# A fused attention and gated-MLP kernel: TensorE's warm-up in short matmuls, and the output weights loaded earlier

## The chip, the cores and the metric

The kernel runs on one core of a Trainium2 chip. The metric is the device time of one execution in microseconds, from start to end. All times below are microseconds unless marked ns. Five engines work side by side, each through its own queue of instructions: TensorE (PE, with its weight loads shown as a row of their own, PEld), VectorE (DVE), ScalarE (ACT), GpSimd (POOL) and SyncE (SP), which in this kernel issues nearly all DMAs.

## What is computed

Two branches read the same normalised input, and the input is added to their sum. S is 2048 rows, D is 640 columns.

```python
xn = layernorm(x)                                  # no scale, no shift
# A: 32 heads of 20 columns, each query sees the 256 keys up to its own
q, k, v = split(xn @ wqkv)
p = softmax(where(0 <= i - j < 256, q @ k.T * 20 ** -0.5, -1e9))
a = (p @ v) @ wo
# B: gated MLP with 1536 hidden columns
b = (sigmoid(xn @ w_gate) * (xn @ w_up)) @ w_down
out = x + a + b                                    # bfloat16
```

## The kernel before

The rows are worked in four chunks of 512 (`NCH`, `CW`). For each chunk the kernel normalises the rows and turns them (xnT, features on partitions); projects Q and K (`proj_block`, L334) and stores them to a scratch in DRAM, from which `spread` (L352) reads them back with the heads placed on partitions 0, 32, 64 and 96; projects V (L364); computes gate and up products (L454, L461) and h; the scores of step after step (`scores`, L530: 16 to 32 small matmuls a step, then one exponential on ACT and masks on POOL); the products with V (`pv`, L561: some 96 small matmuls); and the output sums, down projection (L475) and output projection (L482) into the same PSUM tile, to which DVE adds the input (L486).

PE's order of work is written out by hand. A list of 75 score steps is walked (15 in chunk 0, 20 in each later chunk, five for each pair of head groups); between two steps a `Fill` object hands out other work, piece by piece, from generators that are queued in a fixed order (`qk1`, `v1`, `out0`, `qk2`, ...), by costs in nanoseconds. Every other engine's queue, SP's too, gets its instructions in the order in which this Python program calls them, and runs them in that order; each waits on semaphores for what it needs. SP's DMAs take turns on eight semaphores, so an issue also waits until the DMA eight places ahead of it has landed.

Three places matter for the change.

*The start.* `keep_warm` (L244) issues matmuls of a constant (ones) into a PSUM tile that nothing reads. Ten of 512 columns stand first in PE's queue. Then come the five transposes of row block 0 (L302, `transpose_rows`), which need the block normalised by DVE (L295), one more warm-up matmul, the transposes of row block 1 (normalised by L669), and the first sums, the V projections (L364). Every matmul is two instructions on PE, a weight load and the matmul itself. The warm-up takes two of the four PSUM buffers of the pool `ps_d`.

*Chunk 1's loads.* `g_v(1)` projects V for chunk 1, four row blocks s, and issues loads as it goes: after s = 0 the first half of K (two spreads), after s = 1 the second halves of Q and of K (`spread`, two DMAs of 256 KB each, four in all), after s = 2 `load_wo` (L223), the output weights in twelve small DMAs (L226, L228, L231) of 40 to 100 KB. The second halves are first read in chunk 1's eleventh score step, the output weights by the first output projection of chunk 0 (L482, in `out0`). Behind them in SP's queue stand the stores of chunk 2's normalised rows (L306), the residual rows for `out0` (L492) and the reads of the normalised rows (L313).

*PE's instructions themselves.* The program is unrolled: PE runs 8,717 instructions (8,690 without the waits and branches that stand by themselves), which reach the core by a DMA queue of their own, in packets of 16 KB.

## Time and profile before

| | us |
|---|---|
| median of 3 runs | 309.78 |
| the three runs | 309.49, 309.78, 310.4 |
| the profiled execution | 309.91 |
| its span, first to last instruction | 307.69 |
| TensorE's clock at full speed from | 4.83 |
| first transposes, first V projection | 5.38, 6.81 |
| chunk 1's second halves issued | 73.84 to 75.86 |
| output weights issued, first use of the last of them | 75.89 to 86.8, 89.34 |
| second halves first read | 112.6 |

The profile is of one execution. A row of the timeline has the start, the time that it covers, engine, line, operation, the tiles that it writes and reads, their shape and how many instructions are merged; in brackets stands the idle time of the engine just before and what ended it. The view of the chain follows the work that ended last back from the end and says for each stretch which engine, DMA or issue it went through. The view by stretches gives busy time and count for each engine, then the granted clock of TensorE as a share of full speed, the busy share of the DMA engines and GB/s. A matmul's row includes its latency, so a stream of matmuls is best read by the distance from start to start.

### The profile page before, as it was taken

The numbers are of one execution on the slowest core, as the hardware profiler recorded it, in microseconds if no ns is written. First come the engines' busy times: TensorE is split into PE (matmuls) and PEld (weight loads), VectorE is DVE, ScalarE is ACT, GpSimd is POOL, SyncE is SP. The second block draws the span as 40 slices with busy tenths as digits, with TensorE's granted clock in tenths as the row PEclk, the third lists the DMA queues.
The fourth block names the chain that finished last, engine by engine and source line by source line (L and its number), as shares of the span: only waits on it lengthen the run. The fifth ranks groups of instructions, "written<-read, shape, count | busy, mean of one in ns | idle before, by whom it ended". The sixth has DMA issues, their size and how long they took to land.

```text
span 307.7 us, 10021 instructions
## 1 busy us (share of the span) xinstructions
PE 300.1 (98%) x4309; PEld 168.1 (55%) x4344; DVE 179.8 (58%) x356; ACT 197.4 (64%) x194; POOL 164.2 (53%) x304
## 2 busy tenths in 40 slices
PE   7999999999999999999999999999999999999996
PEld 3654444555657654554457654554546665444774
DVE  5735567889856669683827465382733627372433
ACT  6823868688865648888656538868585547778000
POOL 3020668479883728676572727557382756557000
PEclk9999999999999999999999999999999999999999
DMA  7997979445655154564001222640000200000202
GB/s 203 361 344 242 324 217 285 132 150 163 181 162 133 60 161 140 183 206 84 2 2 47 65 75 92 201 150 2 2 0 4 76 33 23 2 2 2 87 21 66
DMA packets 40148, 36.03 MB, mean 117 GB/s; under 512 B 9001, under 2 KB 39849, under 8 KB 40105
## 3 DMA queue, kind: packets, MB, share of 16 engines
q1 hardware_dynamic: 39240, 34.63, 36.8%
q10 hardware_dynamic: 864, 0.77, 0.9%
q8 instruction: 34, 0.56, 0.8%
q14 instruction: 10, 0.07, 0.1%
HBM read 24.77 MB, written 10.62 MB: 115 GB/s over the span
## 4 chain that ended last, share of the span: by engine, by line
PE 91%; DMA 4%; SPq 1%; issue 1%; ACT 1%; DVE 0%
PE y L475 16%; PE pg L454 16%; PE pu L461 16%; PE pqk L334 14%; PE ps L530 8%; PE y L482 7%; PE pv L364 7%; PE acc L561 6%; DMA kT<-sk 3%; DMA wo<-in_A_wo_dram 1%; DMA xc<-in_A_x_dram 1%; SPq L231 1%; SPq L352 0%; PE pt L302 0%; ACT xn L658 0%
## 5 line engine op out<-in xcount | busy, mean ns | idle before, releaser
L542 POOL TENSOR_SCALAR_AFFINE_SELECT pT<-pT 64x512 bf16<-64x512 bf16 (+1 forms) x252 | 152.7, 606 | 91.6 <-ACT pT L535 80.0
L535 ACT ACTIVATE pT<-ps 128x2048 bf16<-128x2048 f32 x75 | 140.8, 1877 | 59.9 <-PE ps L530 58.9
L465 DVE SCALAR_TENSOR_TENSOR h<-th,pu 128x512 bf16<-128x512 f32 x48 | 32.7, 682 | 56.8 <-PE pu L461 43.0
L461 PE MATMUL pu<-xnT,wu 128*128 128x512 bf16 x230 | 58.9, 380 | 0.7 <-issue 0.3
L454 PE MATMUL pg<-xnT,wg 128*128 128x512 bf16 x225 | 58.3, 380 | 1.2 <-issue 0.6
L475 PE MATMUL y<-wd,h 128*128 128x320 bf16 (+2 forms) x396 | 56.6, 295 | 0.0
L334 PE MATMUL pqk<-xnT,wqkv 128*128 128x512 bf16 x190 | 45.1, 381 | 0.8 <-issue 0.4
L475 PEld LDWEIGHTS <-h 128*128 128x128 bf16 x396 | 36.7, 98 | 15.9 <-issue 2.2
L457 ACT ACTIVATE th<-pg 128x512 f32<-128x512 f32 x48 | 28.6, 596 | 15.3 <-PE pg L454 15.1
L454 PEld LDWEIGHTS <-wg 128*128 128x128 bf16 x240 | 22.3, 98 | 25.6 <-issue 2.0
L461 PEld LDWEIGHTS <-wu 128*128 128x128 bf16 x240 | 22.1, 98 | 25.4 <-issue 1.8
L334 PEld LDWEIGHTS <-wqkv 128*128 128x128 bf16 x200 | 22.5, 119 | 18.8 <-issue 1.2
L530 PE MATMUL ps<-qT,kT 20*64 20x320 bf16 (+4 forms) x1456 | 32.2, 259 | 0.5 <-issue 0.5
L530 PEld LDWEIGHTS <-kT 20*64 20x64 bf16 x1456 | 15.8, 103 | 25.0 <-issue 23.0
L573 DVE STREAM_TRANSPOSE t<-acc 128x512 f32<-128x512 f32 x32 | 21.1, 694 | 13.8 <-PE acc L561 13.8
L486 DVE SCALAR_TENSOR_TENSOR rows<-y,rows 128x320 bf16<-128x320 f32 x30 | 14.2, 483 | 22.5 <-PE y L482 19.7
L364 PE MATMUL pv<-wqkv,xnT 128*128 128x320 bf16 x160 | 25.9, 300 | 0.0
L482 PE MATMUL y<-wo,oc 128*128 128x320 bf16 (+2 forms) x165 | 24.4, 295 | 0.1
L561 PE MATMUL acc<-pT,v 64*32 64x320 bf16 (+4 forms) x1456 | 19.6, 252 | 0.0
L561 PEld LDWEIGHTS <-v 64*32 64x32 bf16 x1456 | 16.3, 91 | 5.8 <-ACT pT L535 1.2
L585 DVE TENSOR_TENSOR on<-t,rec 128x320 bf16<-128x320 f32 (+1 forms) x32 | 18.6, 581 | 1.1
L364 PEld LDWEIGHTS <-xnT 128*128 128x128 bf16 x160 | 14.5, 98 | 8.7 <-issue 1.2
(51 smaller groups left out, 175.3 us busy)
## 6 DMA issues: line engine op xcount, KB each, us to landing
qT<-sq SPq DMA_DIRECT2D x16, 256.0 KB
kT<-sk SPq DMA_DIRECT2D x16, 256.0 KB
sq<-st SPq DMA_DIRECT2D x20, 128.0 KB
sk<-st SPq DMA_DIRECT2D x20, 128.0 KB
out_dram<-rows SPq DMA_DIRECT2D x15, 160.0 KB
wg<-in_B_w_gate_dram SPq DMA_DIRECT2D x4, 480.0 KB
wu<-in_B_w_up_dram SPq DMA_DIRECT2D x4, 480.0 KB
xc<-in_A_x_dram SPq DMA_DIRECT2D x3, 640.0 KB
```

The lines of the kernel that those rows point to most:

```text
L334: nc.tensor.matmul(ps, lhsT=wt[:, m, :], rhs=xnT[c][:, d, :], start=(d == 0), stop=(d == DC - 1))
L364: nc.tensor.matmul(ps[:, 0:HALF], lhsT=xnT[c][:, d, s * P:(s + 1) * P], rhs=wqkv[:, d, 2 * D + hf * HALF:2 * D + (hf + 1) * HALF], start=( ...
L454: nc.tensor.matmul(pg, lhsT=part(wg, d, f), rhs=xnT[c][:, d, :], start=(d == 0), stop=(d == DC - 1))
L457: nc.scalar.activation(out=th, in_=pg, func=TANH, scale=0.5)
L461: nc.tensor.matmul(pu, lhsT=part(wu, d, f), rhs=xnT[c][:, d, :], start=(d == 0), stop=(d == DC - 1))
L465: nc.vector.scalar_tensor_tensor(out=h, in0=th, scalar=1.0, in1=pu, op0=ADD, op1=MULT)
L475: nc.tensor.matmul(y[:, 0:cut[1] - cut[0]], lhsT=ht[c, f][:, s * P:(s + 1) * P], rhs=wd[:, f, cut[0]:cut[1]], start=(f == 0), stop=False)
L482: nc.tensor.matmul(y[:, 0:cut[1] - cut[0]], lhsT=oc[c, m][:, s * P:(s + 1) * P], rhs=wo[:, m, cut[0]:cut[1]], start=False, stop=(m == DC - 1))
L530: nc.tensor.matmul(ps[a * U:(a + 1) * U, i, col * U:(col + n) * U], lhsT=qk["k", kc, o // GH][32 * i:32 * i + DH, o % GH + a, kb * U:(kb + ...
L535: nc.scalar.activation(out=pt[:, :, 0:CW], in_=ps, func=EXP, scale=SCALE)
L542: nc.gpsimd.affine_select(out=view, in_=view, pattern=[[0, HG], [0, n], [sign, U]], compare_op=GE, fill=0.0, base=base, channel_multiplier ...
L561: nc.tensor.matmul(acc[32 * i:32 * i + 32, q * U:(q + n) * U], lhsT=vt[kb][a * U:(a + 1) * U, u, h * VW:h * VW + 32], rhs=pt[a * U:(a + 1) ...
```

## The change

The warm-up becomes 2 matmuls of 512 columns and 34 of 128 ahead of the first transposes (before: 10 of 512), and 7 of 128 between the first and the second transposes (before: 1 of 512). They all write one PSUM tile instead of two. On PE 64 instructions more (32 weight loads and 32 matmuls) stand ahead of the first sums, and one more semaphore wait; from there on PE's order is the same. `load_wo` is called in chunk 1 after s = 1 instead of s = 2, and there the second halves' spreads follow after s = 2 instead of s = 1. In SP's queue the twelve loads change places with the four spreads behind the first half of K; all else keeps its place. Chunks 2 and 3, which do not load the output weights, are unchanged, and so are DVE's, ACT's and POOL's queues.

```diff
-    warm = []
-
-    def keep_warm(n):
-        if len(warm) < 2:
-            warm.append(ps_d.tile([P, CW], FP32, name="pwarm", tag="d"))
+    warm = ps_d.tile([P, CW], FP32, name="pwarm", tag="d")
+
+    def keep_warm(n, width=P):
         for k in range(n):
-            nc.tensor.matmul(warm[-1], lhsT=ones[:, 0:P], rhs=ones, start=(k == 0), stop=(k == n - 1))
-
-    keep_warm(6)
-    keep_warm(4)
+            nc.tensor.matmul(warm[:, 0:width], lhsT=ones[:, 0:P], rhs=ones[:, 0:width], start=(k == 0), stop=(k == n - 1))
+
+    keep_warm(2, CW)
+    keep_warm(34)
...
-            if c == 1 and s == 2:
+            if c == 1 and s == 1:
                 load_wo()
-            if s == 1:
+            if s == (2 if c == 1 else 1):
                 spread("q", c, GH, NG)
                 spread("k", c, GH, NG)
...
-    keep_warm(1)
+    keep_warm(7)
```

## The prediction, made before the changed kernel had run

> **What bounds the kernel now.** I read the page first (busy shares, chain), then the chain and the engines' timelines around the three places that the change touches, then the DMA queues.

> ```profile
> PE 300.1 (98%) x4309; PEld 168.1 (55%) x4344; DVE 179.8 (58%) x356; ACT 197.4 (64%) x194; POOL 164.2 (53%) x304
> ...
> q8 instruction: 34, 0.56, 0.8%
> ...
> PE 91%; DMA 4%; SPq 1%; issue 1%; ACT 1%; DVE 0%
> ```

> PE is busy for 98% of the span and is 91% of the chain: only time in which PE stands still can be won, and anything that delays PE is paid in full. PE's start-to-start times show few such stops: the first 6.8 us, one stop at the output weights, one at 203.8 us. The rest of the "issue" entries are short matmul groups with records missing (216 ns, one matmul). The profiled execution took 309.91 us (span 307.69, 2.22 around it), 0.13 above the median of 309.78. By about 0.3% (0.93 us) this kernel can be told from no change.

> **Part 1: the warm-up.** PE's timeline at the start:

> ```profile
> 0.84 4.27 PE L248 MATMUL pwarm<-const-bfloat16-1.0 128*128 128x512 bf16 x10 [0.84 <-PEq L831]
> 5.38 0.45 PE L302 MATMUL pt<-ident,xn 128*128 128x128 bf16 x5 [0.27 <-DVE xn L295]
> 5.67 0.38 PE L248 MATMUL pwarm<-const-bfloat16-1.0 128*128 128x512 bf16 x1
> 6.52 0.45 PE L302 MATMUL pt<-ident,xn 128*128 128x128 bf16 x5 [0.47 <-DVE xn L669]
> ```

> The ten warm-up matmuls start 427 ns apart (512 columns in a slow clock); the clock record goes to 1.0 at 4.83 us. They end by 5.11, the transposes wait for DVE until 5.33 (they start at 5.38, 56 ns apart, each with its own weight load), the second five wait until 6.47. So PE isn't what decides here. The new warm-up is 2 of 512 (0.85 us, to 1.69) and 34 of 128, each with a weight load. In the slow clock 128 columns are a quarter of 427, 107 ns, if the load hides. That no row shows directly; the nearest are these loads:

> ```profile
> 1.65 0.15 PEld L248 LDWEIGHTS <-const-bfloat16-1.0 128*128 128x128 bf16 x1 [0.28 <-issue]
> ...
> 5.38 0.28 PEld L302 LDWEIGHTS <-xn 128*128 128x128 bf16 x5 [1.02 <-DVE xn L295]
> ```

> A load of 147 ns begins with the matmul before it and ends well inside it; in the fast clock five follow in 0.28 us although one takes 98. So a slow pair costs 107 to 147 ns. At 107: until 4.83, 29.3 pairs; the other 4.7 at 56 ns end at 5.09. At 147: 21.4 pairs, then 12.6 x 56 ns, end 5.54, first transposes 0.16 late, which the wait for DVE's second block (6.47) covers, as 5.54 + 0.28 + 7 x 0.056 = 6.21. The seven short ones between the transposes are 0.39 us where one of 0.22 stood, and fit between 5.67 and 6.47. Cost: 0, hidden by the normalisation chain on DVE and ACT; without that cover 0.16 to 0.3. One PSUM tile is allotted instead of two; the four buffers rotate by one and no wait appears. The gain is also 0: the clock was full before the first transpose. [...]

> **Part 2: the output weights.** SP's queue in chunk 1, and the chain there:

> ```profile
> 73.84 0.98 SPq L352 DMA_DIRECT2D qT<-sq  x2
> 74.86 0.98 SPq L352 DMA_DIRECT2D kT<-sk  x2
> 75.89 1.75 SPq L226 DMA_DIRECT2D wo<-in_A_wo_dram  x4
> 78.22 5.75 SPq L228 DMA_DIRECT2D wo<-in_A_wo_dram  x4
> 84.01 2.82 SPq L231 DMA_DIRECT2D wo<-in_A_wo_dram  x4
> ```

> ```profile
> 86.21 3.08 DMA wo<-in_A_wo_dram
> 89.30 0.04 issue
> 89.34 0.97 PE y L482 x6
> ```

> Four of the twelve small loads wait at issue for the four spreads ahead of them to land (8.28 us for the last). The last load lands at 89.30 and the matmul that needs it starts then. Ten such matmuls take 1.74 us there and 1.53 at 95.55: **0.21 us** of stop, which goes. With the loads first, SP issues them from 73.84; none waits for a spread of the second halves, so they are in around 82 (twelve issues of 0.3 to 0.65, three us to land), 6 us early. What is late next: nothing. The second halves go out some 4 to 6 us later, near 80 instead of 74, and with 8.3 us to land are in by 90; their first readers, the eleventh score step of chunk 1, run at 112.6. Behind them on SP stand the stores of the normalised rows (86.94) and the residual rows (88.83); both were held up by the weights and the same spreads, so they go out no later. Bounds: 0 to -0.21; I take -0.21.

> **Part 3: 64 instructions more.** This is the part that I weigh most.

> ```profile
> 203.47 0.33 PE L530 MATMUL ps<-qT,kT 20*64 20x320 bf16 x4
> 204.33 0.41 PE L530 MATMUL ps<-qT,kT 20*64 20x320 bf16 x20 [0.53 <-issue]
> ```

> A score group of 24 matmuls, 0.43 us everywhere else, takes 1.27 here: **0.85 us** lost in the middle of a group, with no semaphore to wait for. Queue q8 fetched 34 packets of 16 KB for PE's 8717 instructions, so one packet is a page of 256. The stopped weight load is row 5807 in the list of PE's instructions, 5826 with the semaphore waits that the list leaves out. If a page begins there, pages begin at 194 + 256n; the fetches fit, the first at 17.76 with instruction 194 running at 18.05, and the next after the stop at 205.47. A fetch that meets no traffic starts 1.14 us after its boundary (204.33 to 205.47) and takes 0.9 to 1.6. The one before it started at 201.94, 2.95 us after its boundary (198.99), ended at 202.92, and PE went on 1.4 later. It came late because the spreads filled the DMA engines:

> ```profile
> 196.00:197.00 1.00, 1.00 (x22) 0.59 (x22) 0.69 (x1) 0.42 (x2) 0.87 (x3) 1.00 0.03 9
> 197.00:199.00 2.00, 1.95 (x19) 1.00 (x25) 1.40 (x3) 1.98 (x2) 0.57 (x5) 1.00 0.89 277
> 199.00:201.00 2.00, 1.95 (x123) 1.55 (x124) 0.72 (x2) 1.04 (x3) 0.00 (x0) 1.00 0.93 294
> ```

> (last columns: clock, DMA share, GB/s). In the changed program everything behind the warm-up stands 65 places later (64, and one wait), so boundaries fall 65 instructions earlier in the work: this pair at 196.05 and 200.2 instead of 198.99 and 204.33. The request then leaves in the one microsecond with idle DMA engines. Start 197.2, late by 0 to 1.8; end 198.2 to 200.0; usable 199.6 to 201.4, needed at 200.2: a stop of 0 to 1.2 us replaces the 0.85. I take 0.2, nearer to the idle case, since one spread of six is ahead of it. All other new boundaries are at least 3.7 us apart (before, three pairs stood 2.9 to 3.05 apart and none stopped, since PE's sequencer runs ahead of its array: the fetch for a boundary that ran at 92.45 started at 92.13), so I expect no other stop.

> [...]

> **Sum.** 309.91 - 0.21 - 0.85 + 0.2 = 309.05 in the profiled execution's terms; less 0.13, **308.9** as a median.

> **Rivals.**
> - The stop stays: it isn't a page, or comes back at 200.2 at its full bound. For: the place has only 0 to 1.2 us of room. Against: its position and the late fetch. [...] 309.91 - 0.13 - 0.21 = 309.57 if it stays as it is, 0.35 more, 309.92, at the bound. Chance 0.29.
> - The weights gain nothing (another wait ends at 89.3): 308.9 + 0.21 = 309.1. Against: no other row ends there. Chance 0.05.
> - Slower: slow loads don't run beside short matmuls. A pair is then 107 + 147 = 254 ns: 12.4 by 4.83, the other 21.6 at 56 + 98 end at 8.2, the first transposes 2.8 us late, with seven more pairs 3.1; 308.9 + 3.1 = 312.0. It decides from 125 ns a pair on (25 slow and 9 fast just end at 5.33), and is paid above about 150. Against: the loads begin beside the matmul before. Chance 0.06.
> - The forecast: 0.60.

> **Numbers.** Range 308.4 to 310.2: low is both stops gone from the median (308.7) less the 0.3 by which the fastest run shown lies under it; high is the first rival's 309.92 with a late clock switch (0.14) and a warm-up that overruns uncovered (0.16). It leaves out the last rival and the tails. Faster by over 0.3% (under 308.85): a little over half of the forecast, 0.33; within 0.3%: 0.59; slower: 0.08, the last rival and a stop at several boundaries.

> **What would show it.** Right: the first transposes still at about 5.4 with DVE ending their wait; ten wo matmuls in 1.53 us; no stop in the score group at 203.5, every group near 0.43, a fetch starting near 197.3. Wrong: a split score group near 200; warm-up starts over 125 ns apart; a new wait on a spread near 112; a fetch not 65 instructions earlier in the work.

## The result, and the profile after

The changed kernel takes 309.0 us (median of 8 runs, 308.71 to 309.48), the kernel before 309.96 in the same comparison (8 runs, 309.34 to 310.61): a ratio of 0.997, 95% interval 0.9956 to 0.9984. Its profiled execution took 309.21 us, span 306.94, against 309.91 and 307.69. The times of the kernel before spread over 1.3 us here, and over as much as 2.8 us in later sets of runs, those of the changed one over 0.8; this spread turns out to be the point.

In the changed file the lines behind the warm-up stand four lower than before (L530 is L526, L482 is L478, L364 is L360). The lines of its page that answer to those shown of the kernel before:

```profile
PE 303.3 (99%) x4376; PEld 171.8 (56%) x4376; DVE 179.3 (58%) x356; ACT 197.6 (64%) x194; POOL 164.1 (53%) x304
...
q8 instruction: 34, 0.56, 0.8%
...
PE 97%; DMA 2%; SPq 0%; DVE 0%; issue 0%
```

The chain goes through PE for 97% of the span instead of 91%: the DMA of the output weights and the stretch of "issue" are gone from it. What is left of DMA, 2%, is the load of wqkv at the start. (Matmul records are complete in this trace; 35 were missing in the other, so PE's busy time can't be compared directly.)

PE's timeline at the start (start, time covered, what, and in brackets the idle time before):

```profile
0.84 4.64 PE L246 MATMUL pwarm<-const-bfloat16-1.0 128*128 128x512 bf16 x36 [0.84 <-PEq L827]
5.30 0.71 PE L298 MATMUL pt<-ident,xn 128*128 128x128 bf16 x5
5.81 0.95 PE L246 MATMUL pwarm<-const-bfloat16-1.0 128*128 128x128 bf16 x7
6.55 0.58 PE L298 MATMUL pt<-ident,xn 128*128 128x128 bf16 x5
7.18 1.52 PE L360 MATMUL pv<-wqkv,xnT 128*128 128x320 bf16 x10
```

The 34 short warm-up matmuls ran 107 ns apart, a weight load beside each, and no longer than until the transposes could start. But in this execution the clock went to full speed only at 6.84 us (4.83 in the other profile), so the fillers and most of the transposes ran slow: the last transpose starts at 6.92, and at 56 ns a step the first V projection could have followed at 6.98, 0.17 behind the 6.81 of the other profile. It starts at 7.18, because the load of wqkv that it needs landed only at 7.14 (the chain at the start):

```profile
2.17 4.97 DMA wqkv<-in_A_wqkv_dram
7.14 0.04 issue
7.18 1.52 PE pv L360 x10
```

The output projection of chunk 0 before, then after, and after it the score group in which PE had stopped:

```profile
88.57 1.74 PE L482 MATMUL y<-wo,oc 128*128 128x320 bf16 x10
```

```profile
88.87 1.53 PE L478 MATMUL y<-wo,oc 128*128 128x320 bf16 x10
...
203.56 0.43 PE L526 MATMUL ps<-qT,kT 20*64 20x320 bf16 x24
```

Ten matmuls in 1.53 instead of 1.74, and 24 score matmuls in one piece in 0.43 instead of 4 and 20 in 1.27. Laid over each other by the starts of PE's weight loads, the two traces differ by +0.30 us at 13 us (start), +0.24 to 0.30 until 89, +0.09 behind the output weights (-0.21), and -0.76 behind the score group (-0.85); from there to the end nothing more changes. The spans differ by 0.75.

### The profile page after: what moved, and what is told of

Read it like the earlier page. It is cut to its first block, busy times and chain, and to the rows that moved or that the text cites. A ratio compares the mean times of both kernels' runs of the same rounds, so it can differ in the third digit from the quotient of the medians.

```text
span 306.9 us, 10122 instructions
## 1 busy us (share of the span) xinstructions
PE 303.3 (99%) x4376; PEld 171.8 (56%) x4376; DVE 179.3 (58%) x356; ACT 197.6 (64%) x194; POOL 164.1 (53%) x304
## 4 chain that ended last, share of the span: by engine, by line
PE 97%; DMA 2%; SPq 0%; DVE 0%; issue 0%
PE y L471 18%; PE pu L457 17%; PE pg L450 17%; PE pqk L330 15%; PE ps L526 9%; PE pv L360 8%; PE y L478 7%; PE acc L557 6%; DMA wqkv<-in_A_wqkv_dram 2%; SPq L176 0%; PE pt L298 0%; DVE xn L482 0%
## 5 line engine op out<-in xcount | busy, mean ns | idle before, releaser
L457 PE MATMUL pu<-xnT,wu 128*128 128x512 bf16 x240 | 59.8, 380 | 0.0
L450 PE MATMUL pg<-xnT,wg 128*128 128x512 bf16 x240 | 59.8, 380 | 0.0
L330 PE MATMUL pqk<-xnT,wqkv 128*128 128x512 bf16 x200 | 46.0, 381 | 0.0
L526 PE MATMUL ps<-qT,kT 20*64 20x320 bf16 (+4 forms) x1456 | 31.9, 259 | 0.0
L526 PEld LDWEIGHTS <-kT 20*64 20x64 bf16 x1456 | 15.7, 103 | 24.3 <-issue 21.8
L482 DVE SCALAR_TENSOR_TENSOR rows<-y,rows 128x320 bf16<-128x320 f32 x30 | 14.2, 483 | 22.3 <-PE y L478 20.6
L360 PE MATMUL pv<-wqkv,xnT 128*128 128x320 bf16 x160 | 25.8, 300 | 0.0
L478 PE MATMUL y<-wo,oc 128*128 128x320 bf16 (+2 forms) x165 | 24.2, 295 | 0.0
L360 PEld LDWEIGHTS <-xnT 128*128 128x128 bf16 x160 | 14.6, 98 | 8.6 <-issue 1.3
L478 PEld LDWEIGHTS <-oc 128*128 128x128 bf16 x165 | 15.6, 98 | 6.3 <-issue 0.4
```

Of the source, the lines that this page charges most:

```text
L330: nc.tensor.matmul(ps, lhsT=wt[:, m, :], rhs=xnT[c][:, d, :], start=(d == 0), stop=(d == DC - 1))
L360: nc.tensor.matmul(ps[:, 0:HALF], lhsT=xnT[c][:, d, s * P:(s + 1) * P], rhs=wqkv[:, d, 2 * D + hf * HALF:2 * D + (hf + 1) * HALF], start=( ...
L450: nc.tensor.matmul(pg, lhsT=part(wg, d, f), rhs=xnT[c][:, d, :], start=(d == 0), stop=(d == DC - 1))
L457: nc.tensor.matmul(pu, lhsT=part(wu, d, f), rhs=xnT[c][:, d, :], start=(d == 0), stop=(d == DC - 1))
L478: nc.tensor.matmul(y[:, 0:cut[1] - cut[0]], lhsT=oc[c, m][:, s * P:(s + 1) * P], rhs=wo[:, m, cut[0]:cut[1]], start=False, stop=(m == DC - 1))
L526: nc.tensor.matmul(ps[a * U:(a + 1) * U, i, col * U:(col + n) * U], lhsT=qk["k", kc, o // GH][32 * i:32 * i + DH, o % GH + a, kb * U:(kb + ...
```

## The experiments

### The loads' order alone

```diff
-            if c == 1 and s == 2:
+            if c == 1 and s == 1:
                 load_wo()
-            if s == 1:
+            if s == (2 if c == 1 else 1):
```

> The kernel before with the loads' order changed alone; PE's work stands one place later (one wait more). Theory of the pages: the score group at 203.5 still loses 0.6 to 1.0 us in its middle, since the page boundary lies one instruction from where it was; the ten matmuls with the output weights near 88.6 take 1.53 instead of 1.74 us; in all 0.2 us faster. Rival, that the stop at 203.5 came of SP's queue and what it had in flight: the stop goes with the new order, in all 1.0 us faster.

309.71 us (12 runs) beside 309.99 for the kernel before (35 runs); ratio 1.0003, 0.9988 to 1.0018. No gain that can be measured; the 0.2 us that were expected are less than this interval can tell. PE's timeline of its profiled execution, two score groups:

```profile
94.95 0.59 PE L530 MATMUL ps<-qT,kT 20*64 20x320 bf16 x24
...
203.40 0.87 PE L530 MATMUL ps<-qT,kT 20*64 20x320 bf16 x24
```

Both should take 0.43. The second is the known stop, 0.44 long here; the first is another one, 0.16, at the page that begins with instruction 2498, also 194 + 256n. So the new order leaves the stops where they were, and the rival that gave it the gain falls.

### The warm-up alone, and a long warm-up with as many instructions

The first kernel has the changed warm-up and the old order of loads. The second keeps the long matmuls:

```diff
-    keep_warm(6)
-    keep_warm(4)
+    def keep_tiny(n):
+        for k in range(n):
+            nc.tensor.matmul(warm[-1][0:32, 0:32], lhsT=ones[:, 0:32], rhs=ones[:, 0:32], start=(k == 0), stop=(k == n - 1))
+
+    keep_warm(7)
+    keep_warm(1)
+    keep_tiny(34)
```

The one long filler between the transposes stays. (In the next two diffs `...` stands for the same `keep_tiny`.)

> The changed warm-up alone, loads in the old order; PE's work stands 64 places later. Theory of the pages: every score group near 0.43 us, no stop at 203.5, the 0.21 us at the output weights remain; 0.85 us faster, less or more by where the clock switches (up to 0.4). Rival, that the load order did it: the stop at 203.5 remains, no gain.

> The kernel before with eight warm-up matmuls of 512 columns and 34 tiny ones (32 by 32) in place of ten of 512, the one between the transposes as before: the long warm-up kept, but 64 instructions more. Theory of the pages: as in the run with the changed warm-up alone, no stop at 203.5, 0.85 us faster. Rival, that the short matmuls themselves win (a busier TensorE, an earlier full clock): the stop at 203.5 remains and the time is that of before, within 0.2 us.

308.99 us and 308.89 us (12 runs each), beside 309.99 for the kernel before: ratios 0.9976 (0.9963 to 0.999) and 0.9968 (0.9958 to 0.9979). Both have the whole gain, one with short matmuls and one without, both without the new order of loads. The score group in the one, then in the other:

```profile
203.34 0.43 PE L526 MATMUL ps<-qT,kT 20*64 20x320 bf16 x24
```

```profile
203.17 0.43 PE L535 MATMUL ps<-qT,kT 20*64 20x320 bf16 x24
```

What the three kernels share is 64 instructions more. The rival of the short warm-up falls. One thing didn't come as expected: in both, with the old order of loads, the ten matmuls with the output weights took 1.53, not 1.74.

### Twenty instructions more

```diff
-    keep_warm(6)
-    keep_warm(4)
...
+    keep_warm(8)
+    keep_warm(1)
+    keep_tiny(11)
```

> The kernel before with nine warm-up matmuls of 512 columns and 11 tiny ones ahead of the transposes: 20 instructions more. Theory of the pages: the boundaries then fall on the first instructions of the group of P*V matmuls at 198.95 and on the gate group at 202.2; the fetch asked for at 198.95 starts near 201.9 as before and is usable near 204.3, so PE stops for about 2.1 us near 202.2 instead of 0.85 at 203.5: about 1.2 us slower than before. Rival, that the stop has nothing to do with the place in the program: a stop of 0.85 at 203.5 as before, no change within 0.2 us.

310.99 us (12 runs, 308.83 to 313.57) beside 309.99; ratio 1.0024, 0.9998 to 1.0051. By its median it lost 1.0 us, but the interval just takes in no change, and its times lie in three groups, 308.8 to 309.4, 310.3 to 311.2 and 312.8 to 313.6. The three runs of the last group had a granted clock of 0.994 or 0.995, the nine others of 1.0. A clock lower by 0.005 to 0.006 is worth 1.6 to 1.9 us of 311, an estimate, so the last group need not be one more stop; why the clock was lower there, no profile shows. The nine others have a median of 310.82. The profiled execution was the fastest of all, without a stop; its fetch for the page at 201.7 started at 197.46, not at 201.9 (the start of a fetch is that of a packet of 16 KB of queue q8, found by narrowing the window of the DMA view). So the same program was profiled again.

> The same program as the one with 20 more, for another profile: its times were in three groups (308.8 to 309.4, 310.3 to 311.2, 312.8 to 313.6) and the one profiled was the fastest, without a stop. Theory of the pages: a slower execution shows one or two stops of about 2 us, each on a boundary (instruction 194 + 256n of PE), each with a fetch that ended 1.1 to 1.5 us before PE went on. Rival: the time is lost elsewhere, with no stop on a boundary.

311.44 us, and PE's timeline has a stop one matmul ahead of the place that had been worked out:

```profile
201.67 0.71 PE L369 MATMUL pv<-wqkv,xnT 128*128 128x320 bf16 x4
204.60 0.31 PE L369 MATMUL pv<-wqkv,xnT 128*128 128x320 bf16 x1 [2.22 <-issue]
204.74 0.81 PE L459 MATMUL pg<-xnT,wg 128*128 128x512 bf16 x3
```

Five V matmuls (one weight load and one matmul each, 136 ns apart) are cut after the fourth, and PE stands for 2.5 us (2.65 from weight load to weight load, less 0.14). The fifth's weight load is instruction 5826, where a page had begun in the kernel before too, but at other work. The page's fetch started at 202.06 and ended at 203.12; PE went on 1.48 later. Whether the fetch is late differs from one execution of the same program to the next: 197.46 in the one, 202.06 in the other. A second, smaller stop, 0.32 us, stands in this trace at the page that begins with 2498: the score group at 95.03 takes 0.64. Behind it PE ran 0.35 us later than in the other profile, while the spreads went out at the same time (195.2); that this made the fetch late is not shown. The expectation had the place to within a matmul and 2.1 us for 2.5, but took for certain what comes in some executions only.

### A whole page more

```diff
-    keep_warm(6)
-    keep_warm(4)
...
+    keep_warm(1)
+    keep_warm(1)
+    keep_tiny(136)
```

> The kernel before with three warm-up matmuls of 512 columns and 136 tiny ones, so 256 instructions more: one whole page. Theory of the pages: every boundary falls on the same work as in the kernel before, so the stop in the score group near 203.5 is back where the fetch is late, and the times spread like those of before (median near 310, a range of 2 us or more), apart from what the longer or weaker warm-up adds at the start (0 to 1.5 us). Rival, that more instructions or a busier start help as such: a median near 309.0 and a range under 1 us, as with 64 more.

310.71 us (12 runs, 309.77 to 311.9) beside 310.39 for the kernel before (17 runs); ratio 1.0014, 0.9997 to 1.0032. 64 instructions more win, 256 more don't. And the stop is back in the same group, after the same four matmuls:

```profile
204.26 0.33 PE L535 MATMUL ps<-qT,kT 20*64 20x320 bf16 x4
205.14 0.41 PE L535 MATMUL ps<-qT,kT 20*64 20x320 bf16 x20 [0.55 <-issue]
```

It is instruction 6082 now, one page behind 5826. Its trace has another loss, 1.0 us at the start, that the profile of the kernel before does not have: the next V projections wait for a load of wqkv.

```profile
9.67 2.21 PE L369 MATMUL pv<-wqkv,xnT 128*128 128x320 bf16 x15 [0.96 <-DMA wqkv<-in_A_wqkv_dram]
```

Whether its other executions lose this too is not known, and a warm-up with few long matmuls is part of this kernel, so its median alone would not decide; the stop's place does.

### Both kernels profiled again

> The kernel before once more, for its profile: does the stop near 203.5 come back, and when does the clock switch. [...] Rival: no stop at all, and the difference between the kernels lies at the start.

> The changed kernel once more, for its profile: no stop on a boundary, the fetch for the page at 200.2 starting near 196 again. [...]

> The changed kernel for a third profile. No stop on a boundary. [...]

The kernel before took 311.6 us this time, and its trace has two stops on boundaries (PE's timeline):

```profile
96.47 0.42 PE L530 MATMUL ps<-qT,kT 20*64 20x320 bf16 x22
97.19 0.21 PE L530 MATMUL ps<-qT,kT 20*64 20x64 bf16 x2 [0.29 <-issue]
...
205.26 0.33 PE L530 MATMUL ps<-qT,kT 20*64 20x320 bf16 x4
205.98 0.41 PE L530 MATMUL ps<-qT,kT 20*64 20x320 bf16 x20 [0.39 <-issue]
```

0.7 us at the known place, and 0.5 from weight load to weight load at the page that begins with 2498, the place that the kernel with the new order of loads had also shown. The rest of what this execution lost is no stop: 1.0 us more than in the other profile at 56.0, in waiting for chunk 1's turned rows (DVE, L317, which had waited for a DMA itself; the weight load waits 1.38 instead of 0.41), and 0.53 us at the start (first V projection at 7.34). The output weights came in time: 1.53.

The changed kernel took 308.93 and 308.82 us with no stop; its fetches for the page at 200.2 started at 195.3 to 196.0 in all three profiles. The clock switched at 6.17 and 6.21, against 6.84 in the first profile.

### The spreads moved, the program not

```diff
-            if s == 1:
+            if s == 1 and c < 3:
                 spread("q", c, GH, NG)
                 spread("k", c, GH, NG)
...
             outp(c, s, ys, rows)
+            if c == 2 and s == 0:
+                spread("q", 3, GH, NG)
+                spread("k", 3, GH, NG)
```

> The kernel before, PE's work at its old place, but chunk 3's second halves of Q and K issued only after the first row block of chunk 2 has been stored (near 238 us; first read near 253). Theory of the pages: the fetch asked for at 198.95 meets two spreads instead of six, starts before 200.8 and is usable before 203.5: no stop there although the boundary lies where it lay; a stop of up to 0.6 near 95 can still come; 0.5 to 0.9 us faster than before at the median. Rival, that the late fetch isn't due to the spreads: the stop of 0.7 to 0.9 us near 203.5 stays.

309.11 us (12 runs, 308.68 to 309.87) beside 309.72 (23 runs); ratio 0.9984, 0.9971 to 0.9996. PE's timeline, then the stretches behind 199 us, and last the second of them in the kernel before (the last columns are clock, DMA share and GB/s):

```profile
203.65 0.43 PE L533 MATMUL ps<-qT,kT 20*64 20x320 bf16 x24
```

```profile
199.00:201.00 2.00, 2.00 (x124) 1.55 (x123) 0.66 (x2) 1.02 (x4) 0.00 (x0) 1.00 0.52 169
201.00:203.00 2.00, 2.00 (x13) 1.10 (x12) 1.67 (x5) 1.85 (x1) 0.08 (x1) 1.00 0.00 0
```

```profile
201.00:203.00 2.00, 2.00 (x12) 1.10 (x12) 1.67 (x4) 1.68 (x1) 0.25 (x1) 1.00 0.96 320
```

PE's program stands where it stood in the kernel before, with a page beginning at 5826, but the DMA engines are half free from 199 us on and idle from 201 (0.52 and 0.00; before, 0.93 and 0.96). The fetch started at 199.81 instead of 201.94, and PE runs through the boundary, where all four profiled executions with that boundary at that work and the spreads in their old place have a stop. This is one profile, but the twelve runs are faster too, with an interval that leaves out no change. So it is the spreads that make the fetch late, and the late fetch that stops PE.

### The long warm-up with 64 more, and the weights first

This is the kernel with the long warm-up above, with the new order of loads added.

> The long warm-up with 34 tiny matmuls (64 instructions more) and the output weights first: all of the change but the short warm-up. Theory of the pages: no stop on a boundary, as with the change; median between 308.7 and 309.0. If the short warm-up has a worth of its own, this kernel is slower than the changed one by more than 0.2 us; if it costs something (a later full clock), faster by 0.1 to 0.2.

308.88 us (12 runs) beside 309.72 (23 runs); ratio 0.9976, 0.9964 to 0.9987. Between the changed kernel (309.0, 308.93, 308.82), this one, and the one with the old order of loads (308.89) no difference can be measured. No version beat the changed kernel by more than that.

## Why the prediction was right, point by point

308.9 us was forecast and 309.0 measured; the range of 308.4 to 310.2 holds every run of the changed kernel.

- **The stop at a page boundary** was the step that carried the forecast, and it holds. Eight stops in five profiled executions of four kernels lie on instruction 194 + 256n, each 1.2 to 1.5 us behind the end of the page's fetch. In the six profiled executions with 64 or 65 instructions more PE has no such stop. The 0.2 us that the forecast left for a new stop at 200.2 was too much: the fetch starts near 196, not at 197.2, so the page is asked for earlier than I had put it (I took the time at which the boundary's own instruction ran, 196.05). What was missing is that the stop is a matter of chance: 0.85, 0.7, 0.44 and 0.86 us in four executions with the boundary there, 2.5 or nothing with 20 instructions more. And the forecast took the pairs of boundaries some 3 us apart for harmless, since none had stopped PE in the one profile. One of them, near 92 and 95 us, cost 0.53 in the second profile of the kernel before, 0.19 and 0.32 in two of the other kernels (from weight load to weight load); in the changed kernel this pair stands 5.0 us apart, and no profile of it has a stop there. The change takes away a risk at two places rather than a fixed 0.85 at one.
- **The rival that the stop isn't a page** falls by the run with 256 more (the stop of 0.86 us after the same four matmuls, at instruction 6082) and the one with 20 more (2.5 us at instruction 5826, at other work). In the kernel before, the fetch that started 2.95 us behind its boundary (198.99 to 201.94) was followed by a stop of 0.85.
- **The output weights** were sized from one execution at 0.21 us. That is what went between the two profiles, but the old order lost it in one of eight profiles (the other seven show 1.53), because there the last four loads went out later than in any other (from 84.01; from 80.37 to 83.65 in the seven). As a typical worth it was over-sized: near 0.03 us (0.21 / 8), and the kernel with the order alone shows no gain. That nothing else becomes late was right: in the changed kernel SP issued the weights from 73.07 to 81.4 and the four spreads after them, and the stores behind these went out at 85.22 (86.94 before).
- **The warm-up at 0**: a slow pair costs 107 ns, the lower bound taken, so the rival of slow pairs falls. The 0.14 that the range has for a late clock switch is shown by no run. What the runs showed in its place: in the two executions with the switch at 6.84 the first V projections started 0.19 (changed warm-up alone, at 7.00) and could have started 0.17 (changed kernel, 6.98, the estimate above) behind the 6.81 of before. What the forecast had no term for is the load of wqkv that landed at 7.14 and cost 0.2 more in the changed kernel's first profile. It is not the clock's doing: in the kernel with the spreads moved, at full clock from 5.54, the first V projection waited for a load of wqkv until 7.16 too. In the two other profiles of the changed kernel (6.17 and 6.21) the first V projection starts at 6.82 and 6.76, so it cost nothing.
- **The sum** in terms of the profiled execution, 309.05, met 309.21: 0.30 too low at the start (late clock and late load), 0.2 too high at the new boundary, and 0.06 in small differences. That the median came so close is partly luck. It rests on errors of opposite sign: the weights' 0.21 was too much for most executions, the stop near 95 had no term, and the kernel before measured 0.18 more in this comparison (309.96) than in the three runs from which the forecast started.

What stays open: whether short matmuls make the clock switch later. With the short warm-up it came at 6.84, 6.17, 6.84 and 6.21; with eight to ten long ones, in some kernels with tiny ones behind them, at 4.83, 5.94, 5.70, 5.48, 4.18, 6.37, 5.54 and 5.21. Four against eight executions suggest it (the kernel with a whole page more, mostly tiny matmuls, had 6.30); none of the runs was made to decide it, and in the times it is worth at most 0.1 us (308.99 against 308.89).

## What to carry to other kernels

In an unrolled program whose TensorE is busy throughout, a gap in the middle of a group with no semaphore to wait for is worth an instruction count. In this case eight such gaps, of 0.2 to 2.5 us, stood on instruction 194 + 256n, each 1.2 to 1.5 us behind the end of a fetch of 16 KB. Heavy DMA traffic made the fetch late here: with the engines 0.93 and 0.96 busy it started at 201.94 and PE lost 0.85 us, with 0.52 and 0.00 at 199.81 and PE lost nothing. That the dense stretch of small matmuls just before the boundary (256 instructions from 198.99 to 204.33, the stop among them) had a part in it is my reading; no run was made to test it. Moving the program by 64 or 65 instructions took the stop away in six profiled executions, moving the traffic in one; moving the program by 20 made it 2.5 us in one execution and nothing in the other. With short matmuls or with tiny ones, 64 more gave the same time (308.99 and 308.89), and 256 more gave none of it (310.71 beside 310.39): so an edit that adds or removes instructions is compared with one that adds or removes as many without the idea. Read more than one execution before a stop of that kind, or a load that lands just in time, is given a price, and look at what ended the wait before a late start is put down to the clock.

## What the runs showed of the hardware that had not been expected

- In the kernel before, one fetch started 1.14 us after the boundary's instruction ran, where PE had just stood still and the DMA engines were all but idle (204.33 to 205.47; other traffic took 3.3% of their time), and one 2.95 us after it, with six spreads of 256 KB in flight (198.99 to 201.94; DMA share 0.93 to 0.96). In the changed kernel one started 0.2 us before PE's matmul at the boundary ran (195.96 and 196.17), so that fetch did not wait for the matmul. The fetches of 16 KB took 0.9 to 1.6 us in the first profiles of the two kernels, and where PE had stopped, it went on 1.2 to 1.5 us after the last byte.
- The times of one and the same program lay in groups some 2 us apart (308.8 to 309.4, 310.3 to 311.2, 312.8 to 313.6 with 20 instructions more). Two profiled executions, 308.83 and 311.44, differ mainly by stops of 2.5 and 0.32 us; the slowest group goes with a granted clock of 0.994 to 0.995.
- Full clock came 3.3 to 6.0 us after the first matmul (4.18 to 6.84, less 0.84), in thirteen profiled executions.
- A weight load of 128 columns hid beside a matmul of 128 columns in the slow clock as well: in the changed kernel, before the switch at 6.84, 34 pairs ran 107 ns apart, although a load's row has 147.
